# Projecting keys and queries in three f16 passes, and regrouping block sums by DMA, in an attention and MoE kernel

## The chip, the core and the metric

One core of a Trainium2 chip runs the whole program in one launch. Its engines have a queue each and meet at semaphores: PE (matmuls; PEld are its weight loads), DVE (vector), ACT (scalar, activations), POOL (GpSimd), and SP, which here issues every DMA. The metric is the device time of one execution in microseconds, the median of several runs; lower is better.

## The reference

Attention with random features, whose output goes through a two-layer MLP with a squared ReLU:

```python
q, k, v: (8, 8, 576, 64) f32;  w_phi: (64, 128);  w_in: (512, 2048);  w_out: (2048, 512)

def phi(x):
    proj = np.einsum('bhsd,df->bhsf', x, w_phi)
    proj = proj - np.max(np.abs(proj), axis=-1, keepdims=True)
    return np.concatenate([np.exp(proj), np.exp(-proj)], axis=-1)

q_p, k_p = phi(q), phi(k)
kv = np.einsum('bhsf,bhsd->bhfd', k_p, v)
z = np.sum(k_p, axis=2)
num = np.einsum('bhsf,bhfd->bhsd', q_p, kv)
den = np.einsum('bhsf,bhf->bhs', q_p, z)[..., None] + 1e-06
x = (num / den), heads side by side: (4608, 512)
out = np.maximum(x @ w_in, 0.0) ** 2 @ w_out
```

## The kernel before

**Attention** goes by 32 *pairs* of heads (`NPAIR`), four pairs a batch. `kp` and `qp` hold a pair as 128 partitions (2 heads x 64 dimensions) by 576 tokens. The first six pairs (`EARLY`) go through `early(p)`, in a form with more PE work; the others through `visit(i)` and `late(p)`. A visit is one block on PE with three parts: the key projection of pair i+1 (`k_main`: four groups of 128 tokens, the two heads in the two halves of the array's rows, and `k_tail` for the last 64 tokens), the products of keys and values of pair i, and the numerators of pair i-1. The projection takes f32 words: weights are 128 tokens of `k_`, and what moves is `wst`, that is `w_phi`, 128 columns. `late(p)` projects the queries (`q_proj`, here `w_phi` is the weight and 288 tokens move), copies them from PSUM to `pt`, finds their largest magnitude (a reduce over partitions on POOL, into `mx`), subtracts it and takes the exponentials (`qe`).

The **block sums** are of two kinds. `column` adds up the features of all keys (`z`): DVE transposes blocks of 32, reduces them to `z4` (128 x 16), moves four slices of 32 partitions side by side into `za` by copies, reduces them to `zr`, and copies that to the four slices of the column `zc`, which scales the exponentials of the queries for the denominators. `inverse` does the same to the denominators: `d4`, four copies to `da`, a reduce to `dr`, the reciprocals into `dq`, a transpose to `dt`. From there DMAs take the inverse denominators through memory (`rd`) to all partitions (`rb`), DVE multiplies, and ACT and DVE write the token block into the ring as two f16 words (`ring`).

**The MLP** goes by 18 chunks of 256 tokens and 8 blocks of 256 hidden units (`moe(c, f)`): `gemm1` with 24 f16 matmuls of 256 columns (three passes over two f16 words each), the square on ACT and DVE, `gemm2` with f32r and bf16 words. From chunk 15 on a form with fewer products is used. A chunk can start when the ring holds its tokens; the ring holds six chunks.

**The order** is set by a planner: every piece of work is added with its engine, an estimate of its time, what it comes after, the buffers that it uses and a rank (`P.add`), and a simulation of the five queues picks the piece with the lowest rank that can start. A table of numbers (`RANKS`) replaces the ranks of most pieces. On the chip each engine then takes its own queue strictly in that order.

Of the kernel before, what the change touches and what calls it, by code (L numbers as in the profile page):

```python
# [26 lines left out]
F = 128  # L27
# [10 lines left out]
ENDS = 2  # L38
LASTB = C0 * T // S
# [259 lines left out]
def tile_kernel(ctx, tc, qp, kp, vp, w_phi, w_in, w_out, out):  # L299
# [14 lines left out]
    def copy(n, to, of):  # L314

        return (("ACT", out_us(n), lambda: A.activation(out=to(), in_=of(), func=AF.Copy)),  # L316
                ("DVE", dve_us(n), lambda: V.tensor_copy(out=to(), in_=of()), None))
# [8 lines left out]
    wbf, wst = wraw[:, 0:2 * F], wraw[:, 2 * F:]  # L326
    win = [cp.tile([128, KT, FF], F16, name=f"win{i}") for i in range(2)]
# [23 lines left out]
    za_ = tiles(sm, "za", [32, 4, 16], F32, 1, EARLY)  # L351
    zr_ = tiles(sm, "zr", [32, 16], F32, 1, EARLY)
# [9 lines left out]
    td_ = tiles(dr, "td", [2, 128, 128], F32, 2, EARLY)  # L362
    rb_ = tiles(at, "rb", [128, S], F32, 2)
# [253 lines left out]
    def k_main(p, to):  # L617
        for t in range(4):
            for h in range(2):
                PE.matmul(out=to(h)[:, 128 * t:128 * t + 128],  # L620
                          lhsT=k_[p][64 * h:64 * h + 64, 128 * t:128 * t + 128],
                          rhs=wst[64 * h:64 * h + 64, :], start=True, stop=True)

    def k_tail(p, to):
        for h in range(2):
            PE.matmul(out=to[64 * h:64 * h + 64, :], lhsT=k_[p][:, 512:576],  # L626
                      rhs=wbf[:, 128 * h:128 * h + 128], start=True, stop=True)

    def keys(p, main, to, use, tail, to_tail, use_tail, rank):

        R = lambda x: rank + x
        exps[p], sums[p] = [], []
        for h in range(2):
# [8 lines left out]
            o = P.add("ACT", act_us(512), lambda n=n: A.activation(  # L642
                out=e_[n][:, :, 1, :], in_=e_[n][:, :, 0, :], func=AF.Exp, scale=-1.0), [o], [("e", n)], R(0.2))
            exps[p].append(P.add("ACT", act_us(512), lambda n=n: A.activation(  # L644
                out=e_[n][:, :, 0, :], in_=e_[n][:, :, 0, :], func=AF.Exp), [o], [("e", n)], R(0.2)))
# [6 lines left out]
        o = P.add("ACT", act_us(128), lambda: A.activation(  # L652
            out=et_[p][:, 1, :], in_=et_[p][:, 0, :], func=AF.Exp, scale=-1.0), [o], [("et", p)], R(0.5))
        exp_t[p] = P.add("ACT", act_us(128), lambda: A.activation(
            out=et_[p][:, 0, :], in_=et_[p][:, 0, :], func=AF.Exp), [o], [("et", p)], R(0.5))
# [31 lines left out]
    def early(p):  # L687
# [10 lines left out]
        kt = P.add("PE", 0.23, lambda: k_tail(p, to_tail()), [k_load[p]], [("k", p), ("pn", ("k", p))], R(0.3), mode=COLS)  # L698
        keys(p, km, k_to, k_use, kt, to_tail, ("pn", ("k", p)), base)
# [178 lines left out]
    def visit(i):  # L878
# [33 lines left out]
        v = P.add("PE", us, work, after, use, rank, mode=(ROWS if k is not None else COLS, COLS))  # L912
        nums = []
# [25 lines left out]
    def late(p):  # L939
# [7 lines left out]
            out=z4_[p], in_=yt_["z", p - EARLY][:, 0:512].rearrange("p (b x) -> p b x", x=32), op=ALU.add, axis=AX.X),  # L947
            [o], [("yt", ("z", p - EARLY)), ("z4", p)], R(RZ))

        def column():  # L950
            for a in range(4):
                V.tensor_copy(out=za_[p][:, a, :], in_=z4_[p][32 * a:32 * a + 32, :])
            V.tensor_reduce(out=zr_[p], in_=za_[p].rearrange("p a x -> p x a"), op=ALU.add, axis=AX.X)
            for b in range(4):
                V.tensor_copy(out=zc_[p][32 * b:32 * b + 32, :], in_=zr_[p].rearrange("p (j b) -> p b j", b=4)[:, b, :])  # L955

        zc = P.add("DVE", 1.75, column, [o], [("z4", p), ("za", p), ("zr", p), ("zc", p)], R(RZ), lock=4.0)
# [41 lines left out]

        def inverse():  # L1000
            for a in range(4):
                V.tensor_copy(out=da_[p][:, a, :], in_=flat(d4_[p])[32 * a:32 * a + 32, :])
# [200 lines left out]
    def split_out(f, rank):  # L1203
# [141 lines left out]
    def gather(c, g2, kx, x_at, ky, y_at, Q):  # L1345
# [4 lines left out]
        dk = NPAIR + NFP + i  # L1350
# [57 lines left out]
    pool_next = P.add("POOL", 6.2, lambda: None, [], [], -100.0)  # L1408
    for p in range(NPAIR):
# [13 lines left out]
    visit(NPAIR)  # L1423
    square_of.after.append(scale_of[B - 1])
# [24 lines left out]
    ">{8G057RHl0{9F&|&1+kDX7vQ^[qTY]Y0c-DW_b??8`!5({t$f-6lOOh,EQV7xo3/I1jbiN!SJd}Kk?}0flbeYMWzW^4[BQqoM?n"  # L1449
    "d#g>Xxw/yIuYwBl^M:U$<TL/UQs>lVM3=EkUl5e<`ub%z#y!UKwzu&d,c|zvVZs:p4%u=y9=oO(hC;7v^Krkf3A#!;(]c<O:cRC]"  # L1450
    "F?jT`rW#yLT!De#$4{i5=)SZ[8GUT{iLFw_V-6tZVnhNpk0`-,65PM&p!PNV@;;*`B:C!7N)tu:|M-b-z`v^7Mf/hDN+?{U4:f<w"
    "8{=_K&<8#`*fP9Hz!P%22{<o#a!L7p0/?p6(#g:ae36;:I-CS4$S/RK]Q]1r.XFyE;[0+^>=*i@:82-%(=>53Y,|6X6;==BpJh=o"
    "(d/$1Z9,,O)[)(CAkn)/^7Kd/O3g2x@.7n9b,@,wik4rHi*^4|1`*%>a:J?-<-;s.{1Q&O7bACjVBR^aOO.MAxkY,f1PH>;N-gM0"
    "hFah`W<:NI,t@>/nQK.H+xCNWf(W9Q/{!_5c)#>,EM?M224+@S7pJm8C:NFL-<92(;cY#KTI3{Yt?J-6>sJxBRG]%a^7#t5g,B%s"
    "Wl3*A+Za.2BK4((pGNIzhp;-RJ4nFa(1$A7X=?;n@Z9w#{#f0W%Y><1B8Ik&[j4xT7^2O}02_+X$^.A$M<I]^}^Z^!o,y`k4r)U-"
    "PHT^2vEa9`ZBB&-=WWrbPtPK[#oMXWW`MNr^D6k4hXTouSJ=Q+.UL$6@7SS5>SqmEn!7i./Hw^vEp9!gc$DATcRfNF,JC%4Y[E/l"
    "|AYZ{ZxUYPyLA;K+<&xL<eM^X3uE[CM,`}QQp)2^PQa/@W@ftJMtGs:HAh]POr@`78prRD8h202_1o2P>Kkg3a$H[9#A5l!71t88"
    ",)4+o)-X=wZ&.SF#s/ZOD}MQa]42_cUrn2`*0GQE8cL-hH-Xi]WXFw?KpaRVC.GnsB5/@|)=P$9Z9Q%JRmCV?ReI!7ez=%&D%M_["
    "Y91l*1BS<ST/Fx$8EfWcU<M]=lCXTn-w#,>{MX{_!7`*TSJQ>yh|[vC@F!?$uqLGb1!d)TugDc$KBUA9avIO84pAO8s=^JAw3ufL"
    "A_kp_LqZ,8j>P$[UaX_KA,iiL8JOw-X}f{OaO+PHKIQj@!p)Po{L<sP$o+S*T^`WB|pZoen8ZK$(GTh7d/G(Dd^W:yfYGsTGpTHF"  # L1460
# [71 lines left out]
```

## Time and profile before

| | |
|---|---|
| time, median of 3 runs | 1051.44 us (1049.41 to 1053.18) |
| the profiled execution | 1051.1 us, its span 1049.3 us |
| granted TensorE clock, mean | 0.993 |
| DMA | 74.82 MB, mean 71 GB/s |

The span is from the first to the last instruction on the core. Busy times are of the profiled execution. In the page's groups a line number is that of the code before; `po`, `ph`, `pp`, `pn` and `pv` are tiles in PSUM. The chain that ended last has these shares: `ph` (gemm1, L1051) 35%, `po` (gemm2, L1082) 30%, keys and values (L676) 5%, the key projection (L620) 3%.

### The profile page before, as it was taken

The numbers are of one execution on the slowest core, as the hardware profiler recorded it, in microseconds if no ns is written. First come the engines' busy times: TensorE is split into PE (matmuls) and PEld (weight loads), VectorE is DVE, ScalarE is ACT, GpSimd is POOL, SyncE is SP. The second block draws the span as 40 slices with busy tenths as digits, with TensorE's granted clock in tenths as the row PEclk, the third lists the DMA queues.
The fourth block names the chain that finished last, engine by engine and source line by source line (L and its number), as shares of the span: only waits on it lengthen the run. The fifth ranks groups of instructions, "written<-read, shape, count | busy, mean of one in ns | idle before, by whom it ended". The sixth has DMA issues, their size and how long they took to land.

```text
span 1049.3 us, 20133 instructions
## 1 busy us (share of the span) xinstructions
PE 1014.6 (97%) x7888; PEld 726.7 (69%) x7958; DVE 844.8 (81%) x1742; ACT 680.3 (65%) x1213; POOL 154.4 (15%) x78
## 2 busy tenths in 40 slices
PE   7878999999999999999999999999999999999998
PEld 5545666766766767767667677666767676778886
DVE  6897988887888887767986778998887798898643
ACT  6888866666756656566656477586657555775553
POOL 0020111112201111111102013321112011001000
PEclk9997999999999999999999999999999999999999
DMA  9653322121222112212322122212112101000000
GB/s 358 237 170 96 149 77 77 52 68 40 89 57 78 57 55 57 74 52 67 91 58 67 50 76 58 67 25 79 55 53 62 38 23 42 13 21 1 21 22 21
DMA packets 66723, 74.82 MB, mean 71 GB/s; under 512 B 35268, under 2 KB 44100, under 8 KB 64580
## 3 DMA queue, kind: packets, MB, share of 16 engines
q1 hardware_dynamic: 66628, 73.53, 22.4%
q8 instruction: 62, 1.02, 0.4%
q14 instruction: 33, 0.27, 0.1%
HBM read 60.49 MB, written 12.99 MB: 70 GB/s over the span
## 4 chain that ended last, share of the span: by engine, by line
PE 88%; DMA 4%; ACT 4%; DVE 2%; issue 1%; SPq 1%; DVEq 0%; ACTq 0%
PE ph L1051 35%; PE po L1082 30%; PE pv L676 5%; PE pp L620 3%; PE pn L894 3%; PE pv L894 2%; PE po L1327 2%; PE pp L964 2%; DMA k<-in_kp_dram 2%; PE pp L1327 1%; DMA den<-sx 1%; PE pn L964 1%; PE pv L681 1%; PE pn L626 1%; PE pn L1327 1%
## 5 line engine op out<-in xcount | busy, mean ns | idle before, releaser
L1051 PE MATMUL ph<-ring,win 128*128 128x256 f16 x3456 | 391.5, 273 | 0.1
L1051 PEld LDWEIGHTS <-win 128*128 128x128 f16 x3456 | 335.9, 98 | 59.5 <-issue 11.1
L977 POOL PARTITION_ALL_REDUCE mx<-pt x52 | 113.6, 2185 | 553.7 <-ACT pt L316 338.2
L1082 PE MATMUL po<-wh,gh 128*128 128x512 f32 x488 | 156.3, 441 | 0.0
L1063 ACT ACTIVATE r<-ph,cw 128x512 f32<-128x512 f32 x122 | 83.5, 684 | 109.9 <-PE ph L1051 109.0
L1082 PE MATMUL po<-wl,gl 128*128 128x512 bf16 x484 | 125.8, 382 | 0.2
L312 DVE TENSOR_TENSOR gl<-ph,gh 128x512 bf16<-128x512 f32 x122 | 83.1, 682 | 50.4 <-ACT ph L1067 40.5
L1082 PE MATMUL po<-wl,gh 128*128 128x512 bf16 x422 | 113.5, 379 | 5.6 <-issue 3.0
L1082 PEld LDWEIGHTS po<-wh,gh 128*128 128x128 f32 x488 | 92.1, 189 | 28.1
L1065 ACT ACTIVATE gh<-r 128x512 fp32r<-128x512 f32 x122 | 76.6, 628 | 9.9 <-PE po L1082 4.0
L1082 PEld LDWEIGHTS <-gh 128*128 128x128 bf16 x488 | 45.5, 98 | 51.5 <-issue 5.4
L1082 PEld LDWEIGHTS <-gl 128*128 128x128 bf16 x488 | 37.8, 98 | 62.3 <-issue 28.6
L1067 ACT ACTIVATE ph<-r 128x512 f32<-128x512 f32 x122 | 71.7, 588 | 1.0
L676 PE MATMUL pv<-e,v 128*64 128x256 f32 x512 | 63.2, 387 | 2.1 <-ACT e L644 2.1
L991 DVE SCALAR_TENSOR_TENSOR pt<-qe,zc,pt 128x576 f32<-128x576 f32 x52 | 42.3, 815 | 25.4 <-ACT pt L989 24.7
L982 ACT ACTIVATE qe<-qe 128x576 f32<-128x576 f32 x52 | 35.1, 675 | 40.5 <-DVE qe L312 40.4
L312 DVE TENSOR_TENSOR qe<-pt,mx 128x576 f32<-128x576 f32 x52 | 39.7, 764 | 13.8 <-POOL mx L977 12.2
L316 ACT ACTIVATE n<-pn 128x320 f32<-128x320 f32 (+1 forms) x32 | 13.7, 429 | 56.1 <-PE pn L894 55.1
L676 PEld LDWEIGHTS pv<-e,v 128*64 128x64 f32 x512 | 36.5, 140 | 19.0 <-ACT e L644 2.5
L642 ACT ACTIVATE e<-e 128x512 f32<-128x512 f32 x64 | 39.6, 621 | 13.1 <-DVE e L639 12.8
L989 ACT ACTIVATE pt<-qe,zc 128x576 f32<-128x576 f32 x52 | 40.0, 770 | 6.3 <-DVE zc L955 3.4
L995 DVE STREAM_TRANSPOSE yt<-pt 128x576 f32<-128x576 f32 x52 | 40.4, 776 | 1.3
(319 smaller groups left out, 1654.6 us busy)
## 6 DMA issues: line engine op xcount, KB each, us to landing
v<-in_vp_dram SPq DMA_DIRECT2D x32, 320.0 KB
k<-in_kp_dram SPq DMA_DIRECT2D x32, 288.0 KB
q<-in_qp_dram SPq DMA_DIRECT2D x32, 288.0 KB
rb<-rd SPq DMA_DIRECT2D x64, 144.0 KB
out_dram<-o SPq DMA_DIRECT2D x30, 256.0 KB
td<-kvs SPq DMA_DIRECT2D x26, 128.0 KB
kz<-td SPq DMA_DIRECT2D x104, 32.0 KB
j<-in_vp_dram SPq DMA_DIRECT2D x4, 320.0 KB
```

The source lines that it names most:

```text
L312: eng.tensor_tensor(out=out_, in0=a, in1=b_, op=ALU.subtract)
L676: PE.matmul(out=to[64 * h:64 * h + 64, 0:256], lhsT=v_[p][:, t, h, :], rhs=e_[2 * p + h][:, t].rearrange("p s f -> p (s f)"), start=t == 0 ...
L894: PE.matmul(out=to[64 * h:64 * h + 64, :], lhsT=kz_[n][:, 128 * s_ + 64 * h:128 * s_ + 64 * h + 64], rhs=qe_[2 * n + h].rearrange("p (s x) ...
L977: o = P.add("POOL", par_us(S), lambda n=n, h=h: G.partition_all_reduce(mx_[n], pt_[p][:, h, :], channels=128, reduce_op=bass_isa.ReduceOp. ...
L991: o = P.add("DVE", dve_us(S), lambda h=h, qe=qe, y=y: V.scalar_tensor_tensor(out=y(), in0=qe(1), scalar=zc_[p][:, 2 * h + 1:2 * h + 2], in ...
L995: o = P.add("DVE", dve_us(S), lambda n=n, y=y: V.transpose(yt_["y", n - 2 * EARLY], y()), [o], [("pt", p), ("yt", ("y", n - 2 * EARLY))], ...
L1051: PE.matmul(out=ph[:, j, :], lhsT=win[w][:, t, 128 * ff:128 * ff + 128], rhs=ring[half][x][:, t, c0:c0 + T], start=k == 0, stop=k == 3 * K ...
L1063: o = P.add("ACT", act_us(512, 1), lambda: A.activation(out=r_[n], in_=ph_[bank], func=AF.Relu, scale=cw[:, f, 0:1]), [g1], [("ph", bank), ...
L1065: sq = P.add("ACT", act_us(512), lambda: A.activation(out=gh_[n], in_=r_[n], func=AF.Square), [o], [("r", n), ("gh", n)], Q)
L1067: o = P.add("ACT", 0.59, lambda: A.activation(out=ph_[bank], in_=r_[n], func=AF.Square), [o], [("ph", bank), ("r", n)], Q, other=("DVE", 0 ...
L1082: PE.matmul(out=po_[po[i][1]], lhsT=g[:, j, 128 * i:128 * i + 128], rhs=w[:, j, :], start=(f == (NFP - ENDS if last else 0) and (s, j) == ...
L1327: PE.matmul(out=to, lhsT=l()[:, a], rhs=r(slice(b_, b_ + 1))[:, 0], start=(f == 0 and k == 0 and place % 2 == 0), stop=(f == NFP - 1 - END ...
```

## The change

For pairs 12 to 31 (`HALF = 12`) keys and queries are cut into two f16 words before they are projected. `narrow(p)` takes the largest magnitude of the pair's keys and of its queries (ACT with a running sum as the bound, a reduce over partitions on POOL), derives a scale (`kb`), writes the scaled f16 word (ACT, or DVE) and the f16 remainder (DVE). `narrow_weights` does the same to `w_phi` once: `whigh`, and `wlow`, which is written over `wraw` after the last f32 projection. Each projection is then three passes that add up in PSUM: high by high, high by low, low by high (`PARTS`). Its result is larger by a known factor, so the six exponentials of the keys and the three copies of the queries take their scale from `sc`. The f16 words lie in the buffers `k` and `q` (two each), which so hold one pair's raw and narrowed keys in turn.

The regrouping copies of `column` and `inverse`, for pairs 6 to 31, become DMAs through memory: `z4` to `zd`, four DMAs to `zq`, one reduce to `zc`; `d4` to `dd`, one DMA to `da`. `RANKS` is another table.

```diff
-    def copy(n, to, of):
+    def copy(n, to, of, by=None):
+        if by:
+            return (("ACT", out_us(n) + 0.09, lambda: A.activation(out=to(), in_=of(), func=AF.Copy, scale=by())),
+                    ("DVE", dve_us(n), lambda: V.tensor_scalar(out=to(), in0=of(), scalar1=by(), scalar2=None, op0=ALU.mult), None))
...
+    wlow = wraw.bitcast(F16)[:, 0:3 * F]
+    whigh = cp.tile([128, 3 * F], F16, name="whigh")
...
+    def narrow(p, rank):
+        n = raw_of(p)
+        last, uses, raws = [], [("ka", p), ("kb", p), ("sc", p)], {"k": (k_, k_load[p]), "q": (q_, q_load[p])}
+        for i, (tag, (raw, ld)) in enumerate(raws.items()):
+            last.append(P.add("ACT", act_us(S, 1), lambda i=i, raw=raw: A.activation(
+                out=sx_["kq", 2 * p + i].bitcast(BF16)[:, 0:S], in_=raw[n], func=AF.Abs, accum_out=ka_[p][:, i:i + 1]),
+                [ld], [(tag, n), ("sx", ("kq", 2 * p + i)), ("ka", p)], rank))
+        def bound():
+            x = kb_[p]
+            G.partition_all_reduce(x[:, 0:2], ka_[p], channels=128, reduce_op=bass_isa.ReduceOp.max)
+            G.tensor_scalar(out=x[:, 4:6], in0=x[:, 0:2], scalar1=TINY, scalar2=2.0 ** -14, op0=ALU.max, op1=ALU.mult)
+        o = P.add("POOL", par_us(2) + 0.15, bound, last + [pool_next], uses[:2], rank + 0.1, lock=0.0)
+        def bits():
+            x, sc = kb_[p], sc_[p]
+            V.reciprocal(out=x[:, 6:8], in_=x[:, 4:6])
+            V.tensor_tensor(out=sc, in0=x[:, 4:6].unsqueeze(2).to_broadcast([128, 2, 2]),
+                            in1=wback.unsqueeze(1).to_broadcast([128, 2, 2]), op=ALU.mult)
+        o = P.add("DVE", 0.36, bits, [o, whole_of["w"]], uses[1:], rank + 0.1)
+        for i, (tag, (raw, ld)) in enumerate(raws.items()):
...
+            x = P.add("ACT", act_us(S, 1), lambda raw=raw, to=to, by=by: A.activation(
+                out=to()[:, 0], in_=raw[n], func=AF.Copy, scale=by()), [o], key, rank + 0.2 + 0.3 * i, other=(
+                "DVE", dve_us(S), lambda raw=raw, to=to, by=by: V.tensor_scalar(
+                    out=to()[:, 0], in0=raw[n], scalar1=by(), scalar2=None, op0=ALU.mult), 4.0))
+            whole_of[tag, p] = P.add("DVE", dve_us(S), lambda raw=raw, to=to, by=by: V.scalar_tensor_tensor(
+                out=to()[:, 1], in0=raw[n], scalar=by(), in1=to()[:, 0], op0=ALU.mult, op1=ALU.subtract),
+                [x], key, rank + 0.3 + 0.3 * i, lock=4.0)
+
+    PARTS = ((0, whigh), (0, wlow), (1, whigh))
...
     def k_main(p, to):
         for t in range(4):
+            if p >= HALF:
+                for i, (x, w) in enumerate(PARTS):
+                    for h in range(2):
+                        PE.matmul(out=to(h)[:, 128 * t:128 * t + 128],
+                                  lhsT=kq16["k"](p)[64 * h:64 * h + 64, x, 128 * t:128 * t + 128],
+                                  rhs=w[64 * h:64 * h + 64, 2 * F:], start=i == 0, stop=i == 2)
+                continue
...
-            out=z4_[p], in_=yt_["z", p - EARLY][:, 0:512].rearrange("p (b x) -> p b x", x=32), op=ALU.add, axis=AX.X),
+            out=z4_[p].rearrange("p (b j) -> p j b", b=4),
+            in_=yt_["z", p - EARLY][:, 0:512].rearrange("p (j b x) -> p j b x", b=4, x=32), op=ALU.add, axis=AX.X),
...
+        o = P.add("SP", 0.4, lambda: SP.dma_start(zd_[p].rearrange("p b j -> p (b j)"), z4_[p]), [o],
+                  [("z4", p), ("zd", p)], R(RZ), land=1.9, xfer=0.1)
         def column():
-            for a in range(4):
-                V.tensor_copy(out=za_[p][:, a, :], in_=z4_[p][32 * a:32 * a + 32, :])
-            V.tensor_reduce(out=zr_[p], in_=za_[p].rearrange("p a x -> p x a"), op=ALU.add, axis=AX.X)
             for b in range(4):
-                V.tensor_copy(out=zc_[p][32 * b:32 * b + 32, :], in_=zr_[p].rearrange("p (j b) -> p b j", b=4)[:, b, :])
-        zc = P.add("DVE", 1.75, column, [o], [("z4", p), ("za", p), ("zr", p), ("zc", p)], R(RZ), lock=4.0)
+                SP.dma_start(zq_[p][32 * b:32 * b + 32], zd_[p].rearrange("(a x) b j -> b x a j", a=4)[b])
+        o = P.add("SP", 1.6, column, [o], [("zd", p), ("zq", p)], R(RZ), land=1.9, xfer=0.1)
+        zc = P.add("DVE", 0.18, lambda: V.tensor_reduce(
+            out=zc_[p], in_=zq_[p].rearrange("p a j -> p j a"), op=ALU.add, axis=AX.X), [o], [("zq", p), ("zc", p)], R(RZ), lock=4.0)
...
+                if p >= HALF:
+                    for i, (x, w) in enumerate(PARTS):
+                        for h in range(2):
+                            PE.matmul(out=rest(h) if lo else pp_["Q", p][:, h, 0:SH], lhsT=w[64 * h:64 * h + 64, 2 * F:],
+                                      rhs=kq16["q"](p)[64 * h:64 * h + 64, x, lo:lo + SH], start=i == 0, stop=i == 2)
+                    continue
...
+        o = P.add("SP", 0.4, lambda: SP.dma_start(dd_[p], flat(d4_[p])), dens, [("d4", p), ("dd", p)], R(RQ + 1.1),
+                  land=1.9, xfer=0.1)
+        o = P.add("SP", 0.4, lambda: SP.dma_start(da_[p], dd_[p].rearrange("(a x) y -> x a y", a=4)), [o],
+                  [("dd", p), ("da", p)], R(RQ + 1.1), land=1.9, xfer=0.1)
         def inverse():
-            for a in range(4):
-                V.tensor_copy(out=da_[p][:, a, :], in_=flat(d4_[p])[32 * a:32 * a + 32, :])
             V.tensor_reduce(out=dr_[p][:, 0:36], in_=da_[p].rearrange("p a x -> p x a"), op=ALU.add, axis=AX.X)
...
-    ">{8G057RHl0{9F&|&1+kDX7vQ^[qTY]Y0c-DW_b??8`!5({t$f-6lOOh,EQV7xo3/I1jbiN!SJd}Kk?}0flbeYMWzW^4[BQqoM?n"
+    "?H<yH3KD.VY%GfE.)>2b@c-QH5G`Ao/UagUhKjUlSX9FJr[S@:NC:GH>4JCWJ%Jk.[T[H4c>f_MX[OTFH9FfMpH9YVL=_1ZaVU7T"
...
```

What stands in the queues now, at three places. First PE, where a visit begins with the key projection. A row is one instruction, with its line, what it writes and reads, and the shape written; `x8` stands for eight in a row. Before, behind the end of a `gemm2`:

```order
L1082 LDWEIGHTS gl_3413
L1082 MATMUL po_3358<-wl_955,gl_3413 128x512
L620 MATMUL pp_3655<-wraw,k_3099 128x128 x8
L626 MATMUL pn_3664<-wraw,k_3099 64x128 x2
L676 MATMUL pv_3667<-e_3496,v_2038 64x256
```

In the changed kernel the same place, of pair 12 (`k_3314` is the tile of the two f16 words; in each pass the two heads have a load and a matmul of their own):

```order
L1193 MATMUL po_3262<-wl_704,gl_3285 128x512
L696 LDWEIGHTS k_3314
L696 MATMUL pp_3351<-whigh,k_3314 128x128
L696 LDWEIGHTS k_3314
L696 MATMUL pp_3351<-whigh,k_3314 128x128
L696 LDWEIGHTS k_3314
L696 MATMUL pp_3351<-wraw,k_3314 128x128
```

So eight f32 rows, with their loads inside, become 24 loads and 24 matmuls (`wraw` now holds `wlow`), and the two rows of the tail six and six; the rest of the visit stands where it stood.

Second DVE, around the sums. Before:

```order
L952 COPY za_4911<-z_10_4906 32x16 x4
L953 TENSOR_REDUCE zr_4916<-za_4911 32x16
L955 COPY zc_4918<-zr_4916 32x4 x4
L996 TENSOR_REDUCE d_9_4806<-yt_4909 128x18
L1002 COPY da_4955<-d_9_4806 32x36 x4
L1003 TENSOR_REDUCE dr_4960<-da_4955 32x36
L1004 TENSOR_SCALAR dr_4960<-dr_4960 32x36
L1006 RECIPROCAL dq<-dr_4960 32x18 x2
L1007 STREAM_TRANSPOSE dt_4965<-dq 32x64
```

And now:

```order
L1053 TENSOR_REDUCE zc_5602<-zq_5528 128x4
L753 TENSOR_TENSOR es_5605<-ez_5599 128x256
L757 TENSOR_TENSOR es_5605<-es_5605,et_5554 64x256
L748 TENSOR_TENSOR ez_5630<-e_5597 128x512
L753 TENSOR_TENSOR es_5605<-ez_5630 128x256
L757 TENSOR_TENSOR es_5605<-es_5605,et_5554 64x256
L1039 STREAM_TRANSPOSE yt_5663<-es_5605 128x512
L1115 TENSOR_REDUCE dr_5666<-da_5562 32x36
L1116 TENSOR_SCALAR dr_5666<-dr_5666 32x36
L1117 RECIPROCAL dq<-dr_5666 32x2x18
L1118 STREAM_TRANSPOSE dt_5670<-dq 32x64
```

The twelve copies are gone; other work stands between the two sums, which wait for their DMAs.

Third SP, the queue of all DMAs, in the same part of the program. Before:

```order
L1014 DMA rd_4967<-dt_4965 18x32 x2
L612 DMA k_4986<-in_kp_dram 128x576
L929 DMA td_4991<-kvs_4984 128x2x128
L556 DMA v_4993<-in_vp_dram 128x640
L835 DMA rb_4997<-rd_4967 64x576 x2
L934 DMA kz_5034<-td_4991 32x8x32 x4
```

And now:

```order
L1045 DMA zd_5521<-z_11_5517 128x16
L1109 DMA dd_5526<-d_10_5417 128x36
L1050 DMA zq_5528<-zd_5521 32x4x4 x4
L566 DMA v_5559<-in_vp_dram 128x640
L1111 DMA da_5562<-dd_5526 32x4x36
L1024 DMA td_5569<-kvs_5564 128x2x128
L1029 DMA kz_5607<-td_5569 32x8x32 x4
L1125 DMA rd_5677<-dt_5670 18x32 x2
L1045 DMA zd_5700<-z_12_5694 128x16
L928 DMA rb_5708<-rd_5677 64x576 x2
```

Seven more DMAs for each pair stand among the loads and stores, each behind the result that it carries.

More of the change, by code (lines that the diff above doesn't have):

```diff
@@ new lines, in loads, with narrow_weights @@
+        if p >= HALF:
+            narrow(p, rank + 0.5)
+    KN = 2 * NPAIR - HALF
+    raw_of = lambda p: p if p < HALF else 2 * p - HALF
+    kq16 = {"k": lambda p: k_.at(2 * p - HALF + 1, [128, 2, S], F16), "q": lambda p: q_.at(2 * p - HALF + 1, [128, 2, S], F16)}
+    whole_of, wide = {}, []
+    def narrow_weights(rank):
+        wk = [sm.tile([128, 1], F32, name=f"wk{i}") for i in range(4)]
+        o = P.add("ACT", act_us(128, 1), lambda: A.activation(
+            out=whigh[:, 0:F], in_=wst, func=AF.Abs, accum_out=wk[0]), [ld_w], [], rank)
+        o = P.add("POOL", par_us(1), lambda: G.partition_all_reduce(
+            wk[1], wk[0], channels=128, reduce_op=bass_isa.ReduceOp.max), [o, pool_next], [], rank, lock=0.0)
+        def bits():
+            V.tensor_scalar(out=wk[0].bitcast(I32), in0=wk[1].bitcast(I32), scalar1=0x7F800000, scalar2=None, op0=ALU.bitwise_and)
+            V.tensor_scalar(out=wback[:, 0:1], in0=wk[0], scalar1=TINY, scalar2=2.0 ** -14, op0=ALU.max, op1=ALU.mult)
+            V.reciprocal(out=wk[2], in_=wback[:, 0:1])
+            V.tensor_scalar(out=wback[:, 1:2], in0=wback[:, 0:1], scalar1=-1.0, scalar2=None, op0=ALU.mult)
+        o = P.add("DVE", 0.75, bits, [o], [], rank)
+        o = P.add("ACT", act_us(384, 1), lambda: A.activation(out=whigh, in_=wraw, func=AF.Copy, scale=wk[2]), [o], [], rank)
+        low = lambda: sx_["wl", 0].bitcast(F16)[:, 0:3 * F]
+        o = P.add("DVE", dve_us(384), lambda: V.scalar_tensor_tensor(
+            out=low(), in0=wraw, scalar=wk[2], in1=whigh, op0=ALU.mult, op1=ALU.subtract), [o], [("sx", ("wl", 0))], rank, lock=4.0)
+        whole_of["w"] = P.add("DVE", dve_us(384), lambda: V.tensor_copy(out=wlow, in_=low()), [o], [("sx", ("wl", 0))], rank, lock=4.0)
@@ L624, in k_tail @@
     def k_tail(p, to):
+        if p >= HALF:
+            for i, (x, w) in enumerate(PARTS):
+                for h in range(2):
+                    PE.matmul(out=to[64 * h:64 * h + 64, :], lhsT=kq16["k"](p)[:, x, 512:576],
+                              rhs=w[:, 128 * h:128 * h + 128], start=i == 0, stop=i == 2)
+            return
         for h in range(2):
@@ L631, in keys @@
         R = lambda x: rank + x
+        by = lambda s: sc_[p][:, 0, s:s + 1] if p >= HALF else 1.0 - 2.0 * s
+        us = lambda n: act_us(n, int(p >= HALF))
+        scaled = [("sc", p)] if p >= HALF else []
         exps[p], sums[p] = [], []
@@ L641, in keys @@
                 [o], [use[h], ("km", n), ("e", n)], R(0.1))
[L642 to L645, printed above, removed]
+            o = P.add("ACT", us(512), lambda n=n: A.activation(
+                out=e_[n][:, :, 1, :], in_=e_[n][:, :, 0, :], func=AF.Exp, scale=by(1)), [o], [("e", n)] + scaled, R(0.2))
+            exps[p].append(P.add("ACT", us(512), lambda n=n: A.activation(
+                out=e_[n][:, :, 0, :], in_=e_[n][:, :, 0, :], func=AF.Exp, scale=by(0)), [o], [("e", n)] + scaled, R(0.2)))
         o = P.add("DVE", dve_us(128), lambda: V.tensor_reduce(
@@ L651, in keys @@
             [o], [use_tail, ("kmt", p), ("et", p)], R(0.4))
[L652 to L655, printed above, removed]
+        o = P.add("ACT", us(128), lambda: A.activation(
+            out=et_[p][:, 1, :], in_=et_[p][:, 0, :], func=AF.Exp, scale=by(1)), [o], [("et", p)] + scaled, R(0.5))
+        exp_t[p] = P.add("ACT", us(128), lambda: A.activation(
+            out=et_[p][:, 0, :], in_=et_[p][:, 0, :], func=AF.Exp, scale=by(0)), [o], [("et", p)] + scaled, R(0.5))
         for h in range(0 if p < EARLY else 2):
@@ L912, in visit @@
         v = P.add("PE", us, work, after, use, rank, mode=(ROWS if k is not None else COLS, COLS))
+        if k is not None and k < HALF:
+            wide.append(v)
         nums = []
@@ L1423, in tile_kernel @@
     visit(NPAIR)
+    whole_of["w"].after += wide
     square_of.after.append(scale_of[B - 1])
```

165 lines of the change are left out of this document (97 added, 68 removed).

## The prediction

> **What bounds the kernel now.** I read the page first (engine shares and slices), then the busy times by stage, then who waits for whom on PE, and last the chain that ended last, to get the price of one projection.
>
> ```profile
> span 1049.3 us, 20133 instructions
> PE 1014.6 (97%) x7888; PEld 726.7 (69%) x7958; DVE 844.8 (81%) x1742; ACT 680.3 (65%) x1213; POOL 154.4 (15%) x78
> PE   7878999999999999999999999999999999999998
> ```
> ```profile
> 0.00:50.00 50.00, 37.96 (x437) 27.44 (x439) 39.09 (x77) 39.00 (x68) 0.68 (x6) 1.00 0.83 312
> 50.00:100.00 50.00, 38.43 (x403) 22.98 (x400) 44.61 (x68) 41.12 (x74) 9.48 (x4) 0.86 0.42 131
> ...
> 150.00:850.00 700.00, 694.93 (x5118) 485.28 (x5174) 569.30 (x1242) 444.12 (x810) 124.64 (x60) 1.00 0.21 61
> ```
> ```profile
> PE po L1082 <- issue: 3.0, 19, 0.2
> PE po L1082 <- ACT n L316: 0.2, 1, 0.2
> ```
>
> The stage rows give length, then busy time of PE, PEld, DVE, ACT and POOL, then the granted clock. From 150 to 850 us PE is busy for 694.93 of 700 us at clock 1.00, while DVE has 569.30 and ACT 444.12 (81% and 63%). The last two rows are all that PE waited for between 150 and 915 us: 3.2 us. So in that stretch a microsecond of work taken from PE is a microsecond of the kernel, and work added to DVE, ACT, POOL or SP is free as long as it doesn't make PE wait. Only the first 100 us (38 of 50 us busy, twice) are bound by something else. Pairs 12 to 31 are all projected behind the first 150 us (26 pairs' queries from 157 to 869, below).
>
> What a projection costs PE now, from the chain (start, length) and from the timeline of another visit:
>
> ```profile
> 505.86 1.09 PE pp L620 x16
> 506.95 0.37 PE pn L626 x4
> ...
> 541.25 0.69 PE pp L964 x4
> 541.93 0.24 PE pn L964
> 542.17 0.01 PE pv L964
> 542.18 0.24 PE pn L964
> ```
> ```profile
> 398.69 1.16 PE L620 MATMUL pp<-wraw,k 64*128 64x128 f32 x16
> ...
> 403.29 1.03 PE L894 MATMUL pv<-qe,kz 128*64 128x256 f32 x8
> 404.26 5.41 PE L1051 MATMUL ph<-ring,win 128*128 128x256 f16 x48
> ```
> ```profile
> L620 PE MATMUL pp<-wraw,k x432: 272/272/374, 73.1 to 842.7; 64*128 64x128 f32 x144
> L676 PE MATMUL pv<-e,v x512: 378/379/691, 12.6 to 874.1; 128*64 128x256 f32 x171
> L964 PE MATMUL pp<-q,wraw x104: 402/455/508, 157.0 to 868.9; 64*128 64x288 f32 x104
> ```
>
> Keys: 1.09 + 0.37 = 1.46 us a pair. Queries: 0.69 + 0.24 + 0.24 = 1.17 us. An f32 matmul stands there as two, and the two heads run side by side in two halves of the array, so 16 rows are 8 steps. The L620 group lasts 1.16 us; its last matmul takes 0.272, and its first, the one of up to 374 ns, is 0.10 late: seven steps in 0.79 us, **0.112 us a step of 128 columns**. The ten steps of a pair's keys are 1.12 us, and the other 0.34 us are the two changes of tile shape. In the query rows a step of 288 columns is 0.24 us; four of them are 0.97 and the change 0.20.
>
> **The change, part by part.**
>
> *Three f16 passes on PE.* Keys go from 10 steps (8 main, 2 tail) to 15 (12 and 3), queries from 4 steps to 6. No row has an f16 step of 128 columns with 64-row weights, so its price is bounded. From below, the f16 stream L1051 above: 48 matmuls in 5.41 us, the last of 0.27, is 0.109 us per 256 columns, so 0.055 for 128 and 0.123 for 288. From the side of issuing, the densest rows of the trace:
>
> ```profile
> 15.65 1.08 PE L709 MATMUL pv<-e,ones 128*32 128x128 f32 x32
> ```
> ```profile
> L709 PEld LDWEIGHTS pv<-e,ones x192: 106/110/111, 15.7 to 98.2; 128*32 128x32 f32 x192
> L676 PEld LDWEIGHTS pv<-e,v x512: 132/137/231, 12.4 to 873.9; 128*64 128x64 f32 x171
> L620 PEld LDWEIGHTS pp<-wraw,k x432: 182/188/189, 73.1 to 842.6; 64*128 64x128 f32 x144
> L1051 PEld LDWEIGHTS <-win x3456: 95/98/100, 100.1 to 1026.0; 128*128 128x128 f16 x192
> ```
>
> There 32 matmuls go in groups of four: (1.08 - 0.27) / 7 is 0.115 us for four loads and four matmuls, 14 ns an instruction. A pair of f16 steps needs two loads and two matmuls, 0.058 us. The load rows tell whether the weights keep up. In f32 a load grows from 110 to 137 to 188 ns for 32, 64 and 128 columns: 0.83 ns a column over a fixed 83 ns, and L620's loads of 188 ns don't hinder steps of 112 ns, so the fixed part is hidden and only the 107 ns of columns can count. The f16 load of 128 columns takes 98 ns, 15 ns over the fixed part. Hence I take **0.060 us** for an f16 step of 128 columns; the ends are 0.055 and 0.112 (a load of the f32 kind). The quick load also shortens a change of shape: L894's last matmul, of the same shape as L676's, ends at 404.32 in the record, 0.16 us after its 256 columns have passed (0.379 against twice the 0.109 of 256 columns in f16), and the f16 stream starts at 404.26, 0.10 us after them, where the changes to f32 took 0.17 to 0.20. I count 0.10 us less for the key block and for the query block, nothing for the tail.
>
> Keys after: 15 x 0.060 + 0.24 = 1.14 us, 0.32 less. Queries after: 6 x 0.123 + 0.10 = 0.84 us, 0.33 less. Together 0.65 us for each of 20 pairs: **13.0 us**.
>
> The Trainium skill, TensorE: Matmul & The Clock Gate, Weight-path perf modes, says that a weight load is fast when it has 128 columns and is not FP32. By that rule the f16 loads of 64 rows are as quick as L1051's; no run here shows one of 64 rows yet, and it speaks against the second rival below.
>
> *Narrowing on ACT, DVE and POOL* (pairs 12 to 31). Nearest rows:
>
> ```profile
> L563 ACT ACTIVATE sx<-v 128x640 bf16<-128x640 f32 x28 | 20.3, 726 | 13.7 <-DMA v<-in_vp_dram 7.4 <-DMA den<-sx 6.3
> L989 ACT ACTIVATE pt<-qe,zc 128x576 f32<-128x576 f32 x52 | 40.0, 770 | 6.3 <-DVE zc L955 3.4
> L982 ACT ACTIVATE qe<-qe 128x576 f32<-128x576 f32 x52 | 35.1, 675 | 40.5 <-DVE qe L312 40.4
> L991 DVE SCALAR_TENSOR_TENSOR pt<-qe,zc,pt 128x576 f32<-128x576 f32 x52 | 42.3, 815 | 25.4 <-ACT pt L989 24.7
> L952 DVE COPY za<-z 32x16 f32<-32x16 f32 x104 | 22.9, 220 | 1.7
> L1002 DVE COPY da<-d 32x36 f32<-32x36 f32 x104 | 20.3, 195 | 1.7
> L955 DVE COPY zc<-zr 32x4 f32<-32x4 f32 x104 | 19.7, 190 | 2.0
> ```
>
> ACT: two passes for the maximum at about 0.7 us, two scaled copies at 0.77, and 0.095 us (770 less 675) on nine instructions that now take their scale from memory: 3.8 us a pair, 76 us in all. With 26 pairs' queries between 157 and 869 us a pair comes every 27 us, so ACT goes from 63% to about 77%. DVE: two remainders of at most 0.82 us and two tiny ones of 0.19, 2.0 us a pair. Small reduces on POOL go behind its 15%. All of it is covered by PE's own work; uncovered, a pair's chain of about 6 us would stand on the path.
>
> *Block sums by DMA* (pairs 6 to 31). DVE loses twelve copies, 4 x (0.220 + 0.195 + 0.190) = 2.4 us a pair, so with the remainders its load falls a little. In their place come seven issues on SP and four hops through memory:
>
> ```profile
> 408.44 0.38 SPq L929 DMA_DIRECT2D td<-kvs  x1
> 410.27 1.82 SPq L934 DMA_DIRECT2D kz<-td  x4
> ```
>
> A hop like this one lands 1.45 us after its issue, four issues take 1.82 us. So each of the two sums comes 4 to 6 us later than by copies, against the 27 us between pairs. What waits for them is `zc` on ACT and the denominators, then the ring; behind SP's waiting instructions stand the loads of later keys, queries and values. I put this at 0, with an end of 13 us, the whole gain (third rival).
>
> *The new order* also moves the first 150 us, where PE is idle for 24 of the first 100 us. I find no reason for a sign: 0, with 3 us either way.
>
> **Sum.** The profiled execution took 1051.1 us, 0.3 under the median of 1051.44. 1051.1 - 13.0 = **1038.1 us**.
>
> **The rivals.**
> 1. *The weights don't keep up, halfway.* If a matmul waited for the recorded end of its load, a step would be 0.100 us (98 and 2 to start): keys 15 x 0.100 + 0.24 = 1.74, 0.28 more; queries hide it (0.123). 20 x 0.05 = 1 us gained, 1050. Against it: L620's steps of 112 under loads of 188 ns. Values between 0.07 and 0.09 give 1041 to 1047. The Trainium skill, the same page, Back-to-back issue gap, gives 81 ns a matmul at 128 columns for a stream of loads and matmuls; by that estimate the keys gain nothing and the time is 1044.5.
> 2. *The loads of 64 rows go at the f32 rate: slower than before.* Main steps of 0.112, the tail's of 0.060, no quicker change of shape: keys 12 x 0.112 + 3 x 0.060 + 0.34 = 1.86, 0.40 more; queries 6 x 0.123 + 0.20 = 0.94, 0.23 less. 20 x 0.17 = 3.4 us more, 1054.5. It decides from a step of 0.104 us on. For it: the only loads with 64 rows are the slow ones of L620. Against it: those are f32, and their time went with the columns alone in three tile shapes.
> 3. *Attention sets the pace, PE waits at the chunks: no change.* The ring is filled barely in time:
>
> ```profile
> 213.38 0.94 DVE L864 SCALAR_TENSOR_TENSOR ring<-rb,cb,ring 128x384 f16<-128x384 f32 x2
> ```
> ```profile
> 214.92 2.35 PE L1051 MATMUL ph<-ring,win 128*128 128x256 f16 x20
> ```
>    The ring's piece ends at 214.32, and the chunk that needs it starts 0.6 us later. If the longer chains hold attention at its old pace, PE idles what it saves: 1047 to 1054. Against it: 19% of DVE and a quarter of ACT are free, and the ranks place attention by the blocks that PE has done.
> 4. *A visit waits for its narrowed keys.* PE takes its queue in order, so everything waits. From 0.65 us a pair on the gain is gone; behind one POOL reduce (113.6 us in 52, 2.2 each) on half of the pairs it is 22 us, 1060.
>
> ```profile
> L977 POOL PARTITION_ALL_REDUCE mx<-pt x52 | 113.6, 2185 | 553.7 <-ACT pt L316 338.2 <-DVE qe L312 60.0 <-DVE gl L312 55.1
> ```
>    Against it: PE's 3.2 us of waits above, in an order that is planned in the same way.
>
> **Chances.** Forecast 0.62 (its own range 1034 to 1042: steps of 0.055 to 0.070 and the 3 us of the first part); rival 1 between 0.07 and 0.09 us 0.10, at 0.10 us 0.06; rival 2 0.05; rival 3 0.10; rival 4 0.07. About 0.3% (3 us) is what a measurement of this kernel can tell from no change: faster is the forecast, the halfway cases and a part of the third rival, 0.75; the same 0.13; slower 0.12. The range from 1033 to 1051 leaves out rivals 2 and 4 and a part of 3.
>
> **What would show it.** Key groups of the f16 passes 1.1 us long in the chain and query groups 0.84; steps of 0.06 us in the timeline; f16 loads with 64 rows of about 98 ns; PE still over 99% busy from 150 to 850 us; ACT near 77% there, DVE not over 81%; the last query projection some 10 us before 869. Wrong would be: PE rows that wait for DVE's remainders or for `ring`, steps of 0.1 us, or a first chunk that starts far from 100 us.

## The result, and the profile after

| | before | after |
|---|---|---|
| time, median of 4 runs each | 1052.18 us (1049.41 to 1053.18) | **1172.95 us** (1168.27 to 1177.47) |
| the profiled execution, its span | 1051.1 us, 1049.3 us | 1177.5 us, 1175.7 us |
| granted TensorE clock, mean | 0.993 | 0.945 |

The changed kernel takes 1.115 times as long as the one before (95% interval 1.110 to 1.120): 121 us slower, where 13 us faster was forecast.

From the page of the changed kernel, the span, the engines' busy shares, PE's busy tenths in 40 slices and the chain that ended last by engine:

```profile
span 1175.7 us, 21066 instructions
PE 1041.5 (89%) x8238; PEld 729.9 (62%) x8238; DVE 813.8 (69%) x1494; ACT 748.1 (64%) x1332; POOL 172.8 (15%) x119
PE   7788999989999898996888987997769599999998
PE 52%; issue 19%; DVE 13%; ACT 7%; DMA 4%; POOL 4%; SPq 0%; POOLq 0%; DVEq 0%; ACTq 0%
```

No engine became the bound. PE stands for 134.2 us (1175.7 less 1041.5) where it stood for 34.7 before, and 19% of the chain, 223 us, is "issue": time in which an engine stood and the profile shows nothing that it waited for. The busy times of two stretches (length; PE, PEld, DVE, ACT, POOL; granted clock; DMA) show where it begins:

```profile
150.00:250.00 100.00, 100.00 (x760) 69.87 (x759) 77.35 (x145) 68.28 (x127) 20.82 (x11) 1.00 0.25 66
250.00:950.00 700.00, 595.45 (x4464) 402.69 (x4461) 440.48 (x825) 416.43 (x756) 112.39 (x83) 0.92 0.19 51
```

Up to 250 us PE runs full at clock 1.00, as before. From there it is busy for 85% of the time, at clock 0.92. No other engine is nearer to full: DVE has 63%, ACT 59%. What begins at 247 us is told by the instructions of two lines, L663 (the `G.tensor_scalar` that makes the scale in `bound`) and L1086 (the reduce of the queries' maximum), and of L977, that same reduce before (count; least, median and greatest ns; first and last start in us):

```profile
L663 POOLq MODIFY_POOL_CONFIG  x40: 82/83/85, 247.4 to 963.6; - x40
L663 POOL TENSOR_SCALAR kb<-kb x20: 262/262/263, 254.2 to 970.4; 128x2 f32<-128x2 f32 x20
```
```profile
L1086 POOLq MODIFY_POOL_CONFIG  x40: 11/11/21, 146.6 to 971.0; - x40
```
```profile
L977 POOLq MODIFY_POOL_CONFIG  x2: 8/8/8, 150.5 to 150.5; - x2
```

Before, POOL's configuration was changed on the way to these reduces once, at 150.5 us, when its plain operations on the weights were done (one more change stands in the set-up, at 0.9 us; the account of the prediction comes back to it). Now each pair from 12 on has a reduce, a plain TENSOR_SCALAR on two numbers, and again a reduce, and ahead of each change of kind stand two MODIFY_POOL_CONFIG: 40 on the way to the plain operation, and on the way back 38 more than before at L1086 and two at L1247, another reduce. Their records are 8 to 85 ns. What they cost is not in the records. The chain that ended last, in the middle of one pair (start, length), says it:

```profile
330.00 0.68 ACT sx L657 x2
330.68 0.08 issue
330.76 0.38 POOL kb L662
331.14 0.06 POOLq L663 x2
331.20 7.83 issue
339.03 0.27 POOL kb L663
...
339.33 0.04 DVE kb L669
```

Two configuration records in 0.06 us, then 7.83 us of nothing, then the plain operation of 0.27 us, and DVE's reciprocal waits for it. The way back, behind the next pair's scale:

```profile
384.46 2.62 issue
387.08 2.16 POOL mx L1086
389.25 0.02 issue
389.27 0.76 DVE qe L313
390.03 0.74 DVE k L682
390.77 0.05 issue
390.82 1.04 PE pp L696 x20
```

Here the TENSOR_SCALAR was over at 380.88, the reduce `mx` starts 6.2 us later, and PE's key projection waits at the end of that chain. The waits of POOL, DVE and ACT add it up (us in total, times, longest):

```profile
POOL kb L663 <- issue: 139.2, 19, 8.5
POOL mx L1086 <- issue: 48.4, 8, 6.5
```
```profile
DVE kb L669 <- POOL kb L663: 120.6, 17, 9.3
DVE qe L313 <- POOL mx L1086: 68.0, 22, 12.2
```
```profile
ACT qe L1091 <- DVE qe L313: 80.6, 26, 13.2
ACT k L678 <- DVE kb L669: 76.9, 13, 8.3
```

On the way out POOL stands 7.3 us on average (139.2 / 19), on the way back 6.05 us where nothing else kept it longer (48.4 / 8). DVE's queue stands behind L669, ACT's behind DVE's, and PE, whose matmuls follow what these two deliver, idles.

### The profile page after: what moved, and what is told of

It is laid out like the page before. It is cut to its first block, busy times and chain, and to the rows that moved or that the text cites. A ratio compares the mean times of both kernels' runs of the same rounds, so it can differ in the third digit from the quotient of the medians.

```text
span 1175.7 us, 21066 instructions
## 1 busy us (share of the span) xinstructions
PE 1041.5 (89%) x8238; PEld 729.9 (62%) x8238; DVE 813.8 (69%) x1494; ACT 748.1 (64%) x1332; POOL 172.8 (15%) x119
## 4 chain that ended last, share of the span: by engine, by line
PE 52%; issue 19%; DVE 13%; ACT 7%; DMA 4%; POOL 4%; SPq 0%; POOLq 0%; DVEq 0%; ACTq 0%
PE ph L1162 22%; PE po L1193 14%; PE pv L766 3%; POOL mx L1086 3%; PE po L1438 2%; DMA raw2i<-in_w_in_dram 2%; PE pp L1438 1%; PE pn L987 1%; DVE e L729 1%; DVE gl L313 1%; DVE pt L1100 1%; DVE km L726 1%; PE pv L987 1%; DMA q<-in_qp_dram 1%; ACT r L1174 1%
## 5 line engine op out<-in xcount | busy, mean ns | idle before, releaser
L1162 PE MATMUL ph<-ring,win 128*128 128x256 f16 x3456 | 410.0, 279 | 51.1 <-DVE gl L313 37.4
L1162 PEld LDWEIGHTS <-win 128*128 128x128 f16 x3456 | 343.5, 100 | 120.4 <-issue 62.7
L1086 POOL PARTITION_ALL_REDUCE mx<-pt x52 | 115.9, 2228 | 462.2 <-ACT pt L318 195.9
L1193 PE MATMUL po<-wl,gh 128*128 128x512 bf16 x488 | 127.6, 384 | 11.0 <-ACT gh L1176 9.7
L669 DVE RECIPROCAL kb<-kb 128x2 f32<-128x2 f32 x20 | 3.3, 165 | 120.6 <-POOL kb L663 120.6
L678 ACT ACTIVATE k<-k,kb 128x576 f16<-128x576 f32 x20 | 15.5, 773 | 89.5 <-DVE kb L669 76.9
L766 PE MATMUL pv<-e,v 128*64 128x256 f32 x512 | 68.5, 412 | 2.2 <-ACT kz L320 1.1
```

The source lines that it names most:

```text
L766: PE.matmul(out=to[64 * h:64 * h + 64, 0:256], lhsT=v_[p][:, t, h, :], rhs=e_[2 * p + h][:, t].rearrange("p s f -> p (s f)"), start=t == 0 ...
L1086: o = P.add("POOL", par_us(S), lambda n=n, h=h: G.partition_all_reduce(mx_[n], pt_[p][:, h, :], channels=128, reduce_op=bass_isa.ReduceOp. ...
L1162: PE.matmul(out=ph[:, j, :], lhsT=win[w][:, t, 128 * ff:128 * ff + 128], rhs=ring[half][x][:, t, c0:c0 + T], start=k == 0, stop=k == 3 * K ...
L1193: PE.matmul(out=po_[po[i][1]], lhsT=g[:, j, 128 * i:128 * i + 128], rhs=w[:, j, :], start=(f == (NFP - ENDS if last else 0) and (s, j) == ...
```

## The experiments

Theory A: the change of POOL's configuration, twice a pair, is the whole loss, and the rest of the change does what it should. Rivals: the order of the work, the longer chains of the block sums through memory, or the f16 passes themselves cost it.

**The scale on DVE.** One line moves from `bound` (POOL) into `bits` (DVE), in front of the reciprocal; the order of everything else is the same.

```diff
-            G.tensor_scalar(out=x[:, 4:6], in0=x[:, 0:2], scalar1=TINY, ...)   # in bound
+            V.tensor_scalar(out=x[:, 4:6], in0=x[:, 0:2], scalar1=TINY, ...)   # in bits
             V.reciprocal(out=x[:, 6:8], in_=x[:, 4:6])
```

> The change with one instruction moved: the small TENSOR_SCALAR that turns a pair's largest magnitude into its scale (L663) goes from POOL to DVE, so POOL runs nothing but reduces in this stretch and needs no MODIFY_POOL_CONFIG. All queues keep their order. Theory A (each change between a reduce and a plain instruction costs POOL some 6 to 8 us, DVE's next instruction waits for it in order, and PE runs dry): PE gets back what the f16 passes save. Key block 1.07 instead of 1.46 us and query block 0.84 instead of 1.17 as the trace of the change shows them, 20 x 0.72 = 14 us: 1034 to 1043 us. Rival B (the longer chain of the narrowing, the hops of the block sums and the fuller ACT hold attention back, whatever POOL does): still over 1110 us.

Measured: **1037.25 us** (1035.9 to 1039.2), ratio to before 0.9867 (0.9849 to 0.9886). One instruction a pair on POOL was worth 135.7 us, 6.8 a pair, and without it the change is a gain of 1.3%: this version beats both kernels. Busy times of its middle, the wait of PE that adds up to most from 150 to 850 us, and a piece of its chain:

```profile
150.00:850.00 700.00, 695.34 (x5488) 483.28 (x5542) 566.71 (x1054) 513.28 (x932) 135.81 (x80) 1.00 0.24 63
```
```profile
PE po L1193 <- issue: 2.4, 15, 0.2
```
```profile
479.82 0.47 PE pp L1063 x6
480.29 0.12 PE pn L1063
...
480.66 5.35 PE ph L1162 x48
486.00 0.78 PE pp L696 x24
486.78 0.29 PE pn L709 x6
```

**A plain operation on POOL in the kernel before.** Nothing of the change is in it: only a TENSOR_SCALAR on two unread numbers, for pairs 12 to 31, once between the two reduces of a pair's queries, and once behind the second.

```diff
+                if p >= 12 and h == 0:        # the other kernel: h == 1
+                    G.tensor_scalar(out=tick[:, 2:4], in0=tick[:, 0:2], ...)
```

> The kernel before, with one tiny TENSOR_SCALAR on POOL (128 x 2, a scratch tile that nobody reads) put between the two reduces mx of each of the pairs 12 to 31; nothing in f16, no new DMA, same order. Theory A: the second reduce comes 13 to 15 us late (out and back), DVE's next instruction waits for it, and 20 of them cost some 60 to 140 us: 1110 to 1190 us. Rival B (the configuration is the 8 ns that its record shows; the loss is due to the narrowing chain or the DMAs): 1050 to 1054 us.

> As the last one, but the tiny TENSOR_SCALAR stands behind the second reduce of the pair, so the change of configuration and back falls into the stretch in which POOL has nothing to do (27 us between pairs). Theory A (it costs only where a queue waits): 1050 to 1056 us. Theory C (a change of configuration disturbs other engines by itself, through the memory port or the instruction traffic): 1080 us or more.

Measured, one run each: 1157.72 us between the reduces, 106 over before, and 1066.99 us behind them, 16 over. The first one's waits:

```profile
POOL mx L980 <- issue: 90.7, 15, 6.5
POOL tick L982 <- issue: 86.1, 12, 8.2
```
```profile
DVE qe L312 <- POOL mx L980: 112.3, 21, 11.5
```

So the stand belongs to the alternation and not to the narrowing, and its price hangs on who waits. Behind the second reduce nearly all of it falls into POOL's own idle time; that it still costs 16 us was not expected. The second one's waits show where most of it comes from:

```profile
DVE n L1140 <- POOL n L1142: 15.4, 3, 10.9
PE ph L1057 <- DVE gl L312: 13.0, 3, 10.0
```

In one place, at 646 us, the reduce behind the dummy is not the next pair's but one of the MLP's norms (`n`, L1142), for which DVE's queue stands 10.9 us, and PE behind it 10.0.

**A second dummy, in the good version.** The scale stays on DVE, and POOL gets the same unread TENSOR_SCALAR behind the reduce of `kb`, so that nobody waits for its result, only for the reduces behind it.

```diff
             G.partition_all_reduce(x[:, 0:2], ka_[p], channels=128, ...)
+            G.tensor_scalar(out=tick[:, 2:4], in0=tick[:, 0:2], ...)
```

> The first experiment (scale on DVE) with a tiny TENSOR_SCALAR on POOL put back where the change had it, behind the small reduce kb, but on a scratch tile that nobody reads: the change of configuration and back is there, and DVE no longer waits for its result, only for the reduce. Theory A: what stays is the delay of the reduces mx behind it in POOL's queue. If the wait of DVE for the scale was the larger part: 1040 to 1080 us. If the delayed reduces are: 1100 to 1170 us.

Measured, one run: 1135.26 us, 98 over the version without it. By this run about 98 of the 136 us come over the reduces that POOL starts late, and 38 more when DVE also waits for the scale. Its waits say the same:

```profile
DVE qe L313 <- POOL mx L1089: 111.0, 23, 12.8
```

**Half of the pairs.** The even pairs make their scale on POOL, the odd ones on DVE.

```diff
+            if p % 2 == 0:
                 G.tensor_scalar(out=x[:, 4:6], ...)
```

> The changed kernel with the scale on POOL for the ten even pairs from 12 on, and on VectorE for the ten odd ones. Theory A (each pair with the change of POOL's configuration costs the same, 135.7 us / 20 = 6.8 us): 1037 + 68 = 1105, within 1090 to 1120. Rival B (the order has slack that takes the wait of single pairs, and only the sum of neighbours runs over): under 1080. Rival C (a few changes are enough to make attention late once, and the rest is then hidden): over 1130.

Measured: 1116.47 us (1115.02 to 1117.88), ratio 1.0623 (1.0593 to 1.0653). The ten even pairs cost 79 us, 7.9 each, and the other ten bring the remaining 56. That is inside what the proportional theory gave, a little above its middle; there is no sign that the slack between two such pairs absorbs anything.

```profile
POOL kb L664 <- issue: 72.1, 10, 7.9
```

**A fourth pass.** To see whether a microsecond of PE is a microsecond of the good version, every projection gets a pass of low by low words (the products that three passes leave out).

```diff
-    PARTS = ((0, whigh), (0, wlow), (1, whigh))
+    PARTS = ((0, whigh), (0, wlow), (1, whigh), (1, wlow))
```

> The kernel with the scale on VectorE, and a fourth pass (low words times low words) in every projection of pairs 12 to 31; the order of all work is otherwise that of that kernel, so PE alone has more to do. From its rows a pass costs a pair 8 of 24 key matmuls of the 0.78 us, 2 of 6 of the tail's 0.29 us and 4 of 12 of the queries' 0.83 us, 0.26 + 0.10 + 0.28 = 0.64 us, 12.7 us over 20 pairs. Theory A (PE is the bound, a microsecond of PE is one of the kernel): 1047 to 1052 us. Rival B (another engine sets the pace since the narrowing, and PE has slack): 1036 to 1042.

Measured: 1046.69 us (1045.45 to 1048.79), ratio 0.9963 (0.9951 to 0.9975): 9.4 us more than with three passes, 0.3 under the range of theory A. Its middle and its chain:

```profile
150.00:850.00 700.00, 700.00 (x5755) 485.71 (x5752) 557.17 (x1036) 507.63 (x921) 136.13 (x80) 1.00 0.23 62
```
```profile
481.79 0.59 PE pp L1063 x8
...
488.22 1.00 PE pp L696 x32
489.22 0.34 PE pn L709 x8
```

A pass costs 0.27 us on the keys (1.34 against 1.07) and 0.12 + 4 x 0.12 - 3 x 0.12 = 0.24 us on the queries (0.59 and four pieces of 0.12, against 0.47 and three), 10.2 us for 20 pairs. My 12.7 us was too much, since steps and changes of shape don't grow alike; PE's time and the kernel's time agree to a microsecond, and from 150 to 850 us PE doesn't stand at all. PE is the bound.

**The block sums by copies again, in the good version's order.** Every other instruction stands where it stood; the two DMA regroupings are twelve copies and a sum on DVE.

```diff
-        SP.dma_start(zd_[p], z4_[p]); four SP.dma_start(zq_[p], zd_[p]); V.tensor_reduce(zc_[p], zq_[p])
+        four V.tensor_copy(za, z4_[p]); V.tensor_reduce(zr_[p], za); four V.tensor_copy(zc_[p], zr_[p])
-        SP.dma_start(dd_[p], d4_[p]); SP.dma_start(da_[p], dd_[p])
+        four V.tensor_copy(da_[p], d4_[p])
```

> The kernel with the scale on VectorE, its order of all work kept instruction for instruction, but the block sums regrouped by twelve copies and a sum on VectorE instead of by seven DMAs. The copies take 62.9 us and the sum 6.5 us in all in the profile before, so about 65 us more of VectorE, and no wait for the two DMAs. Theory A (the block sums are beside PE's path in either form, since VectorE has room: 81 % busy would become 89 to 90 %): 1036 to 1042. Rival B (at 90 % VectorE is late to PE): 1045 to 1065.

Measured: 1043.9 us (1043.06 to 1044.64), ratio 0.9932 (0.9909 to 0.9954), between what the two theories gave: 6.6 us slower than with the DMAs. Its middle and its chain by engine:

```profile
150.00:850.00 700.00, 696.87 (x5519) 481.17 (x5516) 617.70 (x1329) 506.09 (x922) 135.84 (x80) 1.00 0.21 60
```
```profile
PE 73%; DVE 16%; ACT 6%; issue 2%; DMA 2%; POOL 1%; SPq 0%; DVEq 0%; ACTq 0%; POOLq 0%
```

DVE is at 88% instead of 81%, and the chain runs over it for 16% (1% in the good version). PE's waits for other engines grow from 0.4 to 5.0 us between 150 and 915 us; where the other 2 us go stays open.

**Orders planned anew: three misses and a repair.** Three more kernels had work estimates or pieces changed so that the planner placed everything again with a table of ranks that was made for other work. (a) The changed kernel, with 13.3 us more in the planner's estimate of `bound`:

> The change with its POOL instruction kept, but the planner's estimate for it raised from 0.61 to 13.9 us (out and back), with the same table of ranks, so that the queues are ordered around the delay. Theory A1 (what hurts is that DVE, ACT and PE stand in order behind a result that was planned 7 us earlier): most of the loss comes back, 1038 to 1075 us. A2 (the pair's pipeline has no room for 14 us more, whatever the order): over 1110 us.

Measured, one run: 1211.68 us, slower still. That is in the range of the second theory, but one order, from ranks made for other work, doesn't show "whatever the order". (b) The good version with the block sums by copies as in the kernel before, planned with these estimates:

> f16 projections with the scale on DVE (as the first experiment), but the block sums regrouped by DVE's copies as before; the change's table of ranks, and the planner told of the copies. Theory A (PE's own work is the bound, the block sums are hidden either way): 1035 to 1041 us, like the first experiment. Rival (the change needed the DMAs to free DVE: 2.4 us a pair come back on an engine that had 566.7 of 700 us): 1043 to 1060 us.

Measured: 1142.4 us (1141.56 to 1145.29). (c) The kernel before with only the block sums by DMA, the new DMAs at the rank of what they feed:

> The kernel before with only the block sums changed to DMAs (pairs 6 to 31), f32 projections, the ranks of before; the new DMAs take the rank of what they feed. Theory A: 1049 to 1054 us, no change, for PE's work is the same. Rival 1 (sums that come 4 to 6 us later starve the ring): 1056 us or more. Rival 2 (a freer DVE is worth something on its own): under 1047 us.

Measured: 1110.92 us (1109.92 to 1112.41). In all three PE waits at places that the good version doesn't know; of (c):

```profile
PE ph L1061 <- ACT ring L865: 22.9, 3, 20.5
```

They tell nothing about the parts: (b) holds the same work as the copies in the good version's order, and that took 98 us less. The repair of (c) takes as ranks the times at which the order before starts each piece, so that little moves:

> The kernel before, with the block sums alone regrouped by DMA, and the ranks taken from the times at which the order before starts each operation, so that the plan moves less than with the old table. Theory A (the 1110.92 us of the block sums alone came from the order and not from the DMAs): under 1085 us, and the wait of gemm1 for the ring under 20 us. Rival B (the DMAs themselves cost, by their landing in the chain of a pair): 1095 to 1125.

Measured: 1056.28 us (1056.14 to 1059.17), ratio 1.006 (1.0039 to 1.0081). So 55 us of (c) were its order. The regrouping alone, put into the order before, gains nothing and costs 6 us, though DVE has less to do than before; what of that is the DMAs' and what the order's, which still moved a little, stays open:

```profile
150.00:850.00 700.00, 695.57 (x5127) 481.75 (x5127) 510.43 (x926) 437.92 (x797) 123.20 (x59) 1.00 0.23 62
```

## Why the prediction was wrong, step by step

**The step that failed** is one sentence of the narrowing's part: "Small reduces on POOL go behind its 15%", with the price 0 and "PE's own work" as the cover. POOL's share was right (15%), and no measure of what it costs: `bound` is a reduce and a plain operation on two numbers, and what I had to price was the change between the two kinds. It is 7.3 us out and 6.05 us back each time, and of these 13.4 us some 6.8 a pair arrive in the time, 135.7 us in all. Priced by durations the instruction is 0.26 us. My bound "uncovered, a pair's chain of about 6 us would stand on the path" happened to have the size, but I gave it no weight, and it was made of other instructions.

The Trainium skill, GPSIMD Engine Reference, Instruction dispatch, has a rule of this size: the first call to a freshly loaded POOL kernel pays a load of code of about 6 us that the profile shows as no instruction. The way back agrees (6.05 us, longest 6.5); the way to the plain operation is longer by a microsecond. That each alternation pays anew is not in that rule, and the runs show only that POOL stands, not what it does meanwhile.

In the trace before, the change at 150.5 us was hidden: the reduce behind it started at 159.95 and waited for ACT. The one in the set-up stood in the open, two records and then 8.6 us of "issue":

```profile
masks.py:199 POOLq MODIFY_POOL_CONFIG  x2: 11/11/11, 0.9 to 1.0; - x2
9.52 0.28 POOL masks.py:199 TENSOR_SCALAR_AFFINE_SELECT ident<-ident 128x128 f32<-128x128 f32 x1 [8.59 <-issue]
```

At the start of a program other things may be in such a gap, but the size was there to be asked about, and the count could be read from the order. I did not ask what the new rows on POOL were.

**Rival 4** (a visit waits for its narrowed keys) was the right kind, in order and all: PE takes its queue in order, so everything waits. Its price was wrong, one reduce of 2.2 us on half of the pairs, 1060 us, because the price was read from the duration of a reduce. "Against it: PE's 3.2 us of waits, in an order that is planned in the same way" did not hold: the order was planned with 0.15 us for the plain operation.

**What the version with the scale on DVE shows of the other steps**, at 1037.25 us against 1038.1:

- The f16 step: twelve key steps in 0.78 us of the chain, changes of shape included; 0.057 us a step by the starts of the rows, 0.060 forecast. The loads of 64 rows and 128 columns are quick:

```profile
L696 PEld LDWEIGHTS <-k x480: 92/94/96, 286.2 to 836.7; 64*128 64x128 f16 x160
```

  Rivals 1 and 2 fall with that. The Trainium skill's 81 ns a matmul at 128 columns (TensorE: Matmul & The Clock Gate, Back-to-back issue gap) doesn't hold here, and the measurement decides: two loads and two matmuls of 64 rows, side by side, take 57 ns together.
- Keys 0.78 + 0.29 = 1.07 us (1.14 forecast), queries 0.84, from 479.82 to 480.66 (0.84 forecast): from 2.63 to 1.91 us, 14.4 us for 20 pairs against the 13.0 of the sum.
- "In that stretch a microsecond of work taken from PE is a microsecond of the kernel": PE has 695.34 of 700 us, and the fourth pass cost what it took on PE.
- ACT went to 73% (77% forecast), DVE stayed at 81%, as forecast. Rival 3 fell: PE doesn't wait for the ring there.
- The block sums by DMA, put at 0, are not 0. With the narrowing they give 6.6 us, presumably because the remainders' load on DVE stays off PE's path only if the copies go (the chain runs over DVE for 16% with copies, 1% with DMAs); without it they cost 6 us in the order that was tried. The f16 passes alone would have brought 7 us in this order (1043.9), not 13. The sum came out near because the two parts lean on each other: 14.4 us on PE, of which the copies on DVE would have taken back half. So 1037.25 beside a forecast of 1038.1 is in part luck.

The loss on the changed kernel was then about 101 us of PE standing longer (134.2 against 33.3 us, spans less busy times) and up to 40 us of PE busy longer (1041.5 against 1001.7) with the same work, at a granted clock of 0.945 against 0.988. In the good version's trace 67 matmul records are missing; against the copies in its order, whose trace has the same work and all records (1009.7 us busy), it is 32.

## What to carry to other kernels

Before pricing an instruction by its duration, ask what kind the instructions before and behind it on its engine are: on POOL, a plain operation between two partition reduces cost 6 to 8 us on either side, though it worked on two numbers only, and "15% busy" says nothing of that. A record without a price (here a configuration of 83 ns), or one whose count goes from 4 to 84 in the new order, must be followed to the next instruction of its engine. When part of a change is tested alone in a planned order, keep the order and change the instruction: planning anew moved the time by 39 to 98 us here, more than the parts in question.

## What the hardware showed

- The stand behind a change of POOL's configuration, which no record shows: from the reduce to the plain operation 7.3 us (longest 8.5), back 6.05 us (longest 6.5), against records of 8 to 85 ns.
- The granted clock was lower where PE idled: 1.00 from 150 to 250 us, where PE was full, 0.92 where it was busy for 85%. Of the 141 us over the good version 32 to 40 are PE's own rows that last longer.
